# One core, attention into two mixture layers: the last sequence routed block by block, and work moved between engines inside the attention

## The chip, the cores and the metric

One Trainium2 chip, one of its cores. The metric is the device time of one execution in microseconds (us), lower is better. Times are compared as medians of runs of the same kernel.

## What is computed

Three layers in a row. The first is attention in which a query sees only the keys of its own cluster; the second sends every token to one of eight experts; the third is a dense two-matrix layer with a smooth gate. Cut from the reference:

```python
# attention: q, k, v (2, 8, 768, 64) fp32, 16 centroids per head
q_assign = np.argmax(np.einsum('bhsd,hcd->bhsc', q_n, c_n), axis=-1)   # the same for k
mask = q_assign[:, :, :, None] == k_assign[:, :, None, :]
scores = np.where(mask, scale * np.matmul(q, k.transpose(0, 1, 3, 2)), -1e9)
attn = np.exp(scores - np.max(scores, axis=-1, keepdims=True))
x = np.matmul(attn / (np.sum(attn, axis=-1, keepdims=True) + 1e-09), v)
# x becomes (1536, 512): 2 sequences of 768 tokens, 8 heads side by side
logits = x @ w_gate; expert_idx = np.argmax(logits, axis=1)            # 8 experts
# a token's place = how many earlier tokens went to its expert; dropped from 384 on
out[i] = gate_w[i] * (relu(x[i] @ w1[e]) @ w2[e])                      # 512 -> 1024 -> 512
# last layer: h = x @ w_in (512 -> 2048); g = h * tanh(softplus(h)); g @ w_out
```

## The kernel before

Almost all products are made of 16-bit halves: a value is a high part (fp16) and a low part (what is left), and a product is high times high, low times high and high times low. Some operations are there only to make such parts ("conversions").

**Attention.** There are 16 heads (8 of each sequence) and each head has two blocks of 384 queries, so 32 units u. A unit has three steps (z = 3u + t, 96 steps). For each unit: three score products against the keys that give the row maxima (`maxp`, line 663, copied out by ScalarE as `ev`, line 672, then halved three times, line 679, and reduced, line 683, on VectorE); the maxima are written into the queries and turned by a DMA transpose (`maxfin`, line 710, result `Q`); scores with the maxima in them (`scores`, lines 737 and 738) and their exponentials (line 745, `P`); the low parts of the exponentials (`plo`, line 762, `PL`), one operation for each of four key tiles; the weighted sum of the values (`av`, line 792, in PSUM as `pa`); the division and the split of the result into high and low (`avfin`, lines 815 to 831: `dn`, `x`, `xd`). For each head: the split of q, k and v (lines 517 to 564), the cluster choice (`cluster`, lines 592 to 627), of which `kmask` and `qmask` (lines 624 and 627) write the one-hot masks, and DMA transposes. All PSUM banks of these stages are in two rings, "s" (3 double banks) and "a" (2 banks).

**Routing.** After the last head pair of a block the token logits are put together from four head pairs: three by DMA transposes (`XT`, line 977, product in line 996, sum `LG` in lines 987 and 989), the last by transposes on TensorE (line 1008, copies `XTb` in line 1016, product in line 996, sum in line 1032). `plan_route` then chooses the expert (lines 1076 to 1080), counts places with small products (line 1096), computes the gate weight and the row number (`SLOT`, line 1103), and the Pool engine sends each group of 128 tokens to its row of `xs` in HBM by an indirect DMA (line 1130), six for a sequence. The first sequence is routed block by block while the second is in the attention. The second sequence is routed at the end, both its blocks (six groups) at once.

**One expert ahead.** 112 tokens of the largest expert of the first sequence are computed before the others (`go_ahead`: `phv` line 1597, `hv` lines 1602 and 1605, `pyv` line 1631, `yg` line 1553). Each weight piece (512 KB) is loaded as fp32 (`w1f`, `w2f`, line 1423), turned into a high part on ScalarE (line 1427) and a low part on VectorE (`wl`, line 1435). Eight pieces are needed, four of w1 and four of w2; two of w1 are asked for inside the attention's plan (at z = 86 and 89), the others after it. Then the eight experts follow (`ph` line 1470, `py` line 1515, tokens `xt` read back from `xs` by DMA transposes, line 1398), then the last layer (`fh` line 1785, `po` line 1873).

**What sets the order.** A planner written in the kernel takes the operations in the order of a list and gives each the first gap on its engine that fits, by durations written beside each operation; afterwards all are emitted in the order of their planned starts. So the position of every instruction on every engine is fixed before the program runs, and engines wait for each other by semaphores. The list is ordered by z plus or minus a lead per stage: `lm` (maxima) 8 steps ahead of the scores, `ls` 22, `lc` 16, `plo` 3 steps behind (`lp`), the sums 6 behind (`la`). `plan.best` takes the way that ends first by the planner's durations, after adding a bias. Where TensorE has a planned gap, small dummy products of 232 columns are put in (lines 462 and 466, `<-zero,ones`), and of 512 columns before the first expert (line 1479).

Of the kernel before, what the change touches and what calls it, by code (L numbers as in the profile page):

```python
# [9 lines left out]
F32 = mybir.dt.float32  # L10
# [34 lines left out]
    zs=2, zn=13, rest=300, lsl=1000.0, dsl=400.0, idur=100, iw=232, la=6, lm=8,  # L45
    lc=16, ls=22, ll=30, pt=1, r0=0.45, r1=50.0, nb=5, pb=3,
    qb=5, lp=3, profile=(320, 272, 240, 224, 192, 176, 160, 144), va=(112,), vbias=1000.0, ybias=1000.0, vf=3, vw=4,
    sbias=1000.0, plsl=30000, nl=1, abias=-20000.0, ol=2, wa=4, wb=4, vn=2,
    vz=86, vs=3, hsbias=500.0, obias=1000.0, nwi=4, nw=2, avw=225, fli=44, rsl=6000.0, lag0=5, lags=(), lasti=6, idl=30000, ask=2, pli=12, ob=4, pr=1.0, pr0=1.0, nwo=3, wo0=40, wos=8, hsl=200.0,
# [219 lines left out]
class Builder:  # L269
# [102 lines left out]
    def attention(self, ctx, rctx, pctx, plan, mkeep, extra, then):  # L372
# [200 lines left out]
        def cluster(i, part):  # L573
# [31 lines left out]
            else:  # L605
# [22 lines left out]

                def turn(nm, X, bufs):
# [8 lines left out]
                plan.op("DVE", 100, kmask, use=(e3, bf["KX0", i % nbuf]), add=KXb)  # L638
                plan.op("DVE", 100, qmask, use=(e3, bf["QX0", i % nbuf]), add=QXb)
# [6 lines left out]
        def maxp(u, t):  # L646
# [35 lines left out]
            def last():  # L682
                nc.vector.tensor_reduce(out=mkeep[:, u], in_=st["eh", u][:, :, 0:96], axis=AX.X, op=ALU.max)
# [8 lines left out]
            if t == 2:  # L692
                eh = Buf("eh", 2)
                plan.op("DVE", dve2(3 * 384), halve(384), use=bf["ev", u], new=eh)
                for n in (192, 96):
                    plan.op("DVE", dve2(3 * n), halve(n), use=eh, add=eh)
                plan.op("VEC", dve1(3 * 96), last, use=eh, new=bf["mk", u])
# [54 lines left out]
        def plo(u, pr):  # L752
            for j in range(2):
                kt = 2 * pr + j
                if kt >= NT - NW:
                    continue

                def emit(eng, kt=kt, j=j):
                    def f():
                        if ("PL", u) not in st:  # L760
                            st["PL", u] = late.tile([128, NT - NW, 384], F16, name="PL", tag="PL", bufs=P["pb"])
                        eng.tensor_tensor(out=st["PL", u][:, kt], in0=st["P32", u, pr][:, j], in1=st["PH", u, pr][:, j], op=ALU.subtract)  # L762
                    return f
                a, b = [("DVE", 470, emit(nc.vector))], [("POOL", 956, emit(nc.gpsimd))]
                plan.best(b, a, bias=P["pbias"], use=bf["P32", u, pr], new=bf["PL", u] if kt == 0 else None, add=bf["PL", u])
# [35 lines left out]
        def avfin(u):  # L801
# [4 lines left out]
            if h % 2 == 0 and blk == 0:  # L806
                self.XDb[b, pr] = (Buf(("XH", b, pr), 1), Buf(("XL", b, pr), 1))
            XHb, XLb = self.XDb[b, pr]
# [30 lines left out]
            if h == H - 1:  # L839
                def rest():  # L840
# [7 lines left out]
                    elif blk == BLK - 1:  # L848

                        self.plan_route(plan, b * BLK, BLK, self.small, ps)  # L850
                        self.plan_totals(plan, ps)
                later(rest, u)
            elif blk == BLK - 1:

                groups = [(0, 1, 2)] if b < B - 1 else [(0, 1), (2,)]
                for pairs in groups:
                    if pairs[-1] == pr:
                        fs = self.plan_gate(plan, b, late, ps, pairs=pairs)
                        for k, f in enumerate(fs):
                            later(f, u, k * P["gstep"] - P["defer"] if k < NT else max(0, (NT - 1) * P["gstep"] - P["defer"]))  # L860
# [80 lines left out]
    def plan_gate(self, plan, b, wk, ps, pairs=(), blk=None):  # L941
# [15 lines left out]
        else:  # L957
# [5 lines left out]
            for j in range(2):  # L963
                plan.op("PE", 165, turn[j], use=Xb[j], new=None if j else pm, add=pm)
            plan.op("ACT", act(384) + 55, copy[0], use=pm, new=XT)
            plan.op("VEC", dve1(384), copy[1], use=pm, add=XT)
# [31 lines left out]
    def gate_block(self, b, pr, blk, wk, ps, end):  # L998
# [12 lines left out]
        def copy(a):  # L1011
            def f():
# [3 lines left out]
                nc.vector.tensor_copy(out, src) if a else nc.scalar.activation(out=out, in_=src, func=AF.Copy)  # L1016
            return f

        def mm():
            if end:  # L1020
                pg = t["pm"][:, 0, w:w + 3 * E].rearrange("p (t e) -> p t e", t=3)
                self.pp = t["pm"][:, 1, w:].rearrange("p (t e) -> p t e", t=6)
# [1184 lines left out]
```

## Time and profile before

| | us |
|---|---|
| runs | 700.8, 695.21, 699.46 |
| median | 699.46 |
| profiled execution, its own time | 694.05 |
| span of the profiled execution | 692.3 |
| attention, from start to the last `pa` product | 0 to about 246.5 |
| routing of the last sequence and the expert ahead | 246.5 to 274.2 |
| eight experts | 274.2 to about 426 |
| last layer | 426 to the end |

Over the span TensorE is busy 93%, VectorE 80%, ScalarE 71% and Pool 10%. Busy time overlaps with waiting inside pipelined instructions, so a share says where to look and no more. In the profile PE is TensorE, DVE VectorE, ACT ScalarE, POOL the Pool engine (GpSimd) and SPq the queue of SyncE, which issues most DMAs; PEclk is the granted clock of TensorE, 1.00 for 2.4 GHz and 0.50 for 1.2 GHz.

### The profile page before, as it was taken

What the parts mean: (1) busy time and instruction counts of PE and PEld (TensorE: products, weight loads), DVE (VectorE), ACT (ScalarE), POOL (GpSimd) and SP (SyncE); (2) the same over time, 40 slices, a digit from 0 to 9 for tenths busy, and PEclk for the clock granted to TensorE, in tenths of its full rate; (3) what the DMA queues carried; (4) which work ended last, traced back from release to release, by engine and by line L of the source; (5) the groups of instructions that cost most, each with busy time, mean ns of one, the idle gap of its engine ahead of it and who ended that gap; (6) DMA issues with size and microseconds to landing.
All of it is one profiled execution on the core that took longest, in us unless ns stands there. A gap on an engine that the chain in (4) does not pass through costs nothing. (4 is left out here: it accounts for less than half of the span.)

```text
span 692.3 us, 15431 instructions
## 1 busy us (share of the span) xinstructions
PE 645.5 (93%) x6065; PEld 456.6 (66%) x6065; DVE 554.8 (80%) x1198; ACT 492.5 (71%) x717; POOL 67.2 (10%) x109
## 2 busy tenths in 40 slices
PE   7799999999998966999999999899999999999994
PEld 5576777777776864678999887454555555555541
DVE  6979979999998965788989996889888899545442
ACT  4479979978577723676667675889988878756760
POOL 3200000002200022012000000000260000001303
PEclk9989989999999998999999999999999999999998
DMA  6887999886566258999878992222333221000102
GB/s 176 159 149 191 240 252 226 154 154 190 125 148 106 67 196 254 318 326 295 259 246 257 246 313 95 92 91 62 91 61 94 62 92 32 0 1 16 76 1 95
DMA packets 148961, 103.96 MB, mean 150 GB/s; under 512 B 92304, under 2 KB 131216, under 8 KB 148880
## 3 DMA queue, kind: packets, MB, share of 16 engines
q1 hardware_dynamic: 146576, 96.21, 53.6%
q0 software_dynamic: 2304, 6.69, 2.6%
q8 instruction: 49, 0.80, 0.5%
q14 instruction: 32, 0.26, 0.1%
HBM read 64.02 MB, written 17.51 MB: 118 GB/s over the span
## 5 line engine op out<-in xcount | busy, mean ns | idle before, releaser
L1873 PEld LDWEIGHTS <-gt 128*128 128x128 f16 x576 | 56.3, 98 | 65.1
L745 ACT ACTIVATE P<-s 128x768 f32<-128x768 f32 x96 | 77.8, 812 | 28.6 <-PE s L738 22.5
L1873 PE MATMUL po<-xd,gt 128*128 128x512 f16 x432 | 97.0, 379 | 0.0
L1785 PE MATMUL fh<-x2h,winh 128*128 128x384 f16 x256 | 84.3, 329 | 4.9 <-DVE hs L1804 3.0
L1470 PE MATMUL ph<-xt,wh 128*128 128x320 f16 (+7 forms) x512 | 82.8, 259 | 3.3 <-DMA xt<-xs 3.3
L1785 PE MATMUL fh<-x2l,winh 128*128 128x384 f16 x256 | 84.2, 329 | 0.0
L1785 PE MATMUL fh<-x2h,winl 128*128 128x384 f16 x256 | 84.1, 329 | 0.0
L1515 PE MATMUL py<-ht,wh 128*128 128x320 f16 (+7 forms) x512 | 82.3, 256 | 0.1
L1785 PEld LDWEIGHTS <-winh 128*128 128x128 f16 x512 | 50.4, 98 | 41.9 <-issue 6.8
L672 ACT ACTIVATE ev<-pm 128x768 f16<-128x768 f32 x87 | 70.1, 809 | 7.5 <-PE pm L663 7.3
L737 PE MATMUL s<-Q,KXT 81*128 81x384 f16 x192 | 64.2, 335 | 7.8 <-DMA Q<-QX 5.4
L1470 PE MATMUL ph<-xt,wl 128*128 128x320 f16 (+7 forms) x256 | 64.4, 259 | 2.1 <-DVE wl L1435 2.1
L1515 PE MATMUL py<-ht,wl 128*128 128x320 f16 (+7 forms) x256 | 63.8, 256 | 1.4 <-DVE wl L1435 1.3
L738 PE MATMUL s<-QKT 128*128 128x384 f16 x192 | 64.1, 334 | 0.0
L762 DVE TENSOR_TENSOR PL<-P 128x384 f16<-128x384 f32 x119 | 61.8, 558 | 0.0
L792 PE MATMUL pa<-VW,P 128*128 128x65 f32 x384 | 59.6, 279 | 1.2 <-DVE LG L989 0.5
L792 PEld LDWEIGHTS pa<-VW,P 128*128 128x128 f32 x384 | 54.2, 198 | 8.0 <-issue 2.1
L1470 PEld LDWEIGHTS <-wh 128*128 128x128 f16 x512 | 48.0, 99 | 5.5 <-issue 0.4
L1515 PEld LDWEIGHTS <-wh 128*128 128x128 f16 x512 | 47.6, 98 | 4.9 <-issue 0.3
L792 PE MATMUL pa<-VX,P 128*128 128x65 f16 x768 | 49.6, 196 | 0.0
L663 PE MATMUL pm<-KXT,QXT 80*128 80x384 f16 x192 | 48.3, 335 | 0.8 <-ACT KXT L448 0.5
L792 PEld LDWEIGHTS <-P 128*128 128x128 bf16 x768 | 48.3, 106 | 0.0
(278 smaller groups left out, 1393.6 us busy)
## 6 DMA issues: line engine op xcount, KB each, us to landing
w1f<-in_moe_w_dram SPq DMA_DIRECT2D x36, 512.0 KB, 4.8
w2f<-in_moe_w_dram SPq DMA_DIRECT2D x36, 512.0 KB, 5.2
w2s<-in_moe_w_in_dram SPq DMA_DIRECT2D x16, 512.0 KB, 5.5
w2s<-in_moe_w_out_dram SPq DMA_DIRECT2D x16, 512.0 KB, 3.4
xs<-zero SPq DMA_DIRECT2D x13, 576.0 KB, 4.0
xsave<-xd SPq DMA_DIRECT2D x12, 256.0 KB, 4.3
kf<-in_k_dram SPq DMA_DIRECT2D x7, 384.0 KB, 4.4
qf<-in_q_dram SPq DMA_DIRECT2D x7, 384.0 KB, 4.8
```

The source lines that it names most:

```text
L663: nc.tensor.matmul(pm[:, j, 0:384], lhsT=QXT[0:80, g], rhs=KXT[0:80, 3 * j:3 * j + 3].rearrange("c t p -> c (t p)"), start=True, stop=True)
L672: nc.scalar.activation(out=st["ev", u][:, t].rearrange("p (a c) -> p a c", a=2), in_=st["pm", u, t][:, :, 0:384], func=AF.Copy, scale=1.0 ...
L737: nc.tensor.matmul(s[:, j, 0:384], lhsT=KXT[0:81, kt], rhs=Q2[0:81].rearrange("c t p -> c (t p)"), start=True, stop=False)
L738: nc.tensor.matmul(s[:, j, 0:384], lhsT=QKT[:, 1, kt], rhs=QKT[:, 0, 3 * blk:3 * blk + 3].rearrange("c t p -> c (t p)"), start=False, stop ...
L745: nc.scalar.activation(out=st["P32", u, pr], in_=st["s", u, pr][:, :, 0:384], func=AF.Exp, scale=sc)
L762: eng.tensor_tensor(out=st["PL", u][:, kt], in0=st["P32", u, pr][:, j], in1=st["PH", u, pr][:, j], op=ALU.subtract)
L792: nc.tensor.matmul(pa[:, t], lhsT=lhs, rhs=rhs, start=(n == 0), stop=(n == len(mm) - 1))
L1470: nc.tensor.matmul(st["p", i], lhsT=w[:, kk, fs], rhs=xt[:, 2 * kk + a], start=(kk == 0 and n == 0), stop=(kk == KD - 1 and n == 2))
L1515: nc.tensor.matmul(py, lhsT=w[:, f2, dsl], rhs=x, start=(f == 0 and j == 0), stop=(f == NF - 1 and j == 2))
L1785: nc.tensor.matmul(ph[b][:, 0:HB], lhsT=t2[w][:, f, k // 3], rhs=t2["x2"][x][:, k // 3, c0:c0 + HB], start=(k == 0), stop=(k == 3 * KD - 1))
L1873: nc.tensor.matmul(t2["o"][k], lhsT=gt[:, a, ts_], rhs=t2["wo"][f][:, w], start=(first and j == 0), stop=(last and j == 2))
```

## The change

- `plo` makes the low parts of two key tiles in one VectorE operation (768 elements instead of 384) and no longer has a way on Pool.
- The two masks of each head may go to ScalarE, with a bias that leaves them there unless it ends 1.5 us later.
- The maxima: `lm` 9 for 8; the last halving of 96 elements is dropped, and the reduction takes 192 instead of 96 elements for each of three rows. `plo` is placed 2 steps behind the scores for 3.
- The last sequence: each block has a route of its own (three groups), with its own dependency on the parts of `xd` that it reads. The copies `XTb` go to the engine that ends first.
- The expert ahead: four w1 pieces are placed in the attention (z = 80, 83, 86, 89), with five instead of four buffers for the parts; its first four products are planned ahead of the last route; the logits of the third head pair are placed half a step later.

```diff
-    ..., la=6, lm=8,
+    ..., la=6, lm=9,
-    qb=5, lp=3, ..., vw=4,
+    qb=5, lp=2, ..., vw=5,
-    ..., ol=2, wa=4, wb=4, vn=2,
-    vz=86, vs=3, ...
+    ..., ol=2, mbias=1500.0, glate=0.5, vpool=1000.0, ssl=0, wa=4, wb=4, vn=4,
+    vz=80, vs=3, ...
...
+                def kmask_a():
+                    nc.scalar.activation(out=KX[i % nbuf][:, :, 64:80], in_=st["e3", i][:, 1], func=AF.Copy, scale=KB, bias=-KB)
...
-                plan.op("DVE", 100, kmask, use=(e3, bf["KX0", i % nbuf]), add=KXb)
-                plan.op("DVE", 100, qmask, use=(e3, bf["QX0", i % nbuf]), add=QXb)
+                plan.best([("ACT", 190, kmask_a)], [("DVE", 100, kmask)], bias=P["mbias"], ...)
+                plan.best([("ACT", 190, qmask_a)], [("DVE", 100, qmask)], bias=P["mbias"], ...)
...
-                nc.vector.tensor_reduce(out=mkeep[:, u], in_=st["eh", u][:, :, 0:96], axis=AX.X, op=ALU.max)
+                nc.vector.tensor_reduce(out=mkeep[:, u], in_=st["eh", u][:, :, 0:192], axis=AX.X, op=ALU.max)
-                for n in (192, 96):
+                for n in (192,):
...
-            for j in range(2):
-                kt = 2 * pr + j
-                        eng.tensor_tensor(out=st["PL", u][:, kt], in0=st["P32", u, pr][:, j], in1=st["PH", u, pr][:, j], op=ALU.subtract)
-                a, b = [("DVE", 470, emit(nc.vector))], [("POOL", 956, emit(nc.gpsimd))]
-                plan.best(b, a, bias=P["pbias"], ...)
+            n = min(2, NT - NW - 2 * pr)
+                nc.vector.tensor_tensor(out=st["PL", u][:, 2 * pr:2 * pr + n], in0=st["P32", u, pr][:, 0:n], in1=st["PH", u, pr][:, 0:n], op=ALU.subtract)
+            plan.op("DVE", dve1(384 * n), emit, ...)
...
-                    elif blk == BLK - 1:
-                        self.plan_route(plan, b * BLK, BLK, self.small, ps)
-                        self.plan_totals(plan, ps)
-                later(rest, u)
+                    else:
+                        if blk == BLK - 1 and self.va:
+                            next(then)
+                        self.plan_route(plan, b * BLK + blk, 1, self.small, ps)
+                        if blk == BLK - 1:
+                            self.plan_totals(plan, ps)
+                later(rest, u, 3 * (NU - u) + P["la"] - P["defer"] - 2 if b == B - 1 and blk < BLK - 1 else 0)
...
-            plan.op("ACT", act(384) + 55, copy[0], use=pm, new=XT)
-            plan.op("VEC", dve1(384), copy[1], use=pm, add=XT)
+            for j in range(2):
+                plan.best([("ACT", act(384) + 55, copy(j, "ACT"))], [("VEC", dve1(384), copy(j, "VEC"))], ...)
```

What the order of the instructions became at three places. First TensorE, where the last unit's weighted sum (`pa`, from `P_4732` and `P_4677` before, line 792) stands against the logits of the third head pair (`pg`). Before, the end of the 18 `pg` products and the start of the last `pa`:

```order
L996 LDWEIGHTS XT
L996 MATMUL pg<-WG,XT 128x8
L792 MATMUL pa<-VW_169,P_4732 128x65 x2
L792 LDWEIGHTS P_4677
L792 MATMUL pa<-VX_163,P_4677 128x65
```

In the changed kernel, the end of the last `pa` and the start of `pg`:

```order
L795 MATMUL pa<-VX_163,P_4579 128x65
L795 LDWEIGHTS PL
L795 MATMUL pa<-VX_163,PL 128x65
L1002 LDWEIGHTS XT
L1002 MATMUL pg<-WG,XT 128x8
```

The 18 products moved from ahead of the last unit's sums to behind them. Second VectorE in the routing of the last sequence (`POS`, `OVER`, `rsf`, `SLOT` lead to the row numbers; `t...` are the totals of all experts; `hv` is the expert ahead). Before:

```order
L1099 TENSOR_TENSOR rpm<-pm,OH 128x48
L1121 CAST xd<-rsm 128x6
L1233 SCALAR_TENSOR_TENSOR tce<-pm,vc 128x8
L1122 TENSOR_TENSOR xd<-rsm,xd 128x6
L1100 TENSOR_REDUCE POS<-rpm 128x6
L1234 TENSOR_SCALAR tce<-tce 128x8
L1101 TENSOR_SCALAR OVER<-POS 128x6
L1235 TENSOR_TENSOR tkey<-tce,e_105 128x8
L1102 TENSOR_TENSOR rsf<-POS,rs_5007 128x6
L1103 TENSOR_TENSOR SLOT<-rsf,OVER 128x6
```

In the changed kernel, the end of the first block's route and the start of the second's:

```order
L1107 TENSOR_SCALAR OVER<-POS 128x3
L1127 CAST xd<-rsm 128x3
L1108 TENSOR_TENSOR rsf<-POS,rs_4822 128x3
L1128 TENSOR_TENSOR xd<-rsm,xd 128x3
L1109 TENSOR_TENSOR SLOT<-rsf,OVER 128x3
L1116 TENSOR_TENSOR CS<-CS,OH 128x8
L1082 TENSOR_REDUCE rmx<-LG 128x3
L1083 TENSOR_TENSOR re<-LG,rmx 128x24
L1084 TENSOR_TENSOR re<-re,w_103 128x24
L1612 SCALAR_TENSOR_TENSOR hv<-phv,hv 128x448
```

The row numbers of three groups now come before the second block's choice, and a second `SLOT` of three groups 14 instructions behind this piece. Third the DMA queue of SyncE at the end of the attention. Before:

```order
L1423 DMA w1f<-in_moe_w_dram 128x4x256
L710 DMA_TRANSPOSE Q_4553<-QX_150 128x3x128
L977 DMA_TRANSPOSE XT<-xd 128x2x128 x6
L1423 ISA
L1423 DMA w2f<-in_moe_w_dram 128x2x512
L1423 ISA
L1423 DMA w2f<-in_moe_w_dram 128x2x512
L1137 DMA xsave<-xd 128x1024 x6
L1423 ISA
L1423 DMA w2f<-in_moe_w_dram 128x2x512
```

In the changed kernel:

```order
L1429 DMA w2f<-in_moe_w_dram 128x2x512
L716 DMA_TRANSPOSE Q_4427<-QX_150 128x3x128
L1429 ISA
L1429 DMA w2f<-in_moe_w_dram 128x2x512
L1429 ISA
L1429 DMA w2f<-in_moe_w_dram 128x2x512
L983 DMA_TRANSPOSE XT<-xd 128x2x128 x6
L1143 DMA xsave<-xd 128x1024 x6
L1429 ISA
L1429 DMA w2f<-in_moe_w_dram 128x2x512
```

Three of the four w2 pieces are asked for ahead of the last logits' transposes, and one is left behind the saves, where two were.

## Rows read from the trace of the kernel before

**Rows 1.** windows: us, then busy us (instructions) of PE, PEld, DVE, ACT, POOL; PEclk, DMA, GB/s

```profile
40.00:246.00 206.00, 197.07 (x2602) 156.50 (x2601) 186.86 (x575) 165.52 (x271) 12.16 (x12) 0.97 0.76 168
246.00:274.17 28.17, 16.63 (x272) 14.14 (x272) 19.45 (x60) 9.83 (x15) 7.85 (x6) 0.94 0.70 231
274.17:692.30 418.13, 399.44 (x2889) 263.00 (x2888) 317.24 (x477) 296.75 (x388) 37.46 (x27) 0.99 0.45 135
35.60:42.00 6.40, 6.40 (x47) 3.98 (x45) 5.03 (x16) 4.96 (x9) 0.00 (x0) 0.50 0.67 122
90.00:96.40 6.40, 6.34 (x56) 5.41 (x54) 4.96 (x15) 3.44 (x7) 0.00 (x0) 0.50 1.03 271
```

**Rows 2.** VectorE groups by shape, 20 to 246: count, busy us, mean ns, idle before

```profile
L762 DVE TENSOR_TENSOR PL<-P 128x384 f16<-128x384 f32 x119 | 61.8, 558 | 0.0
...
L683 DVE TENSOR_REDUCE mkeep<-eh 128x3 f32<-128x288 f16 x29 | 13.1, 453 | 0.7
L831 DVE TENSOR_TENSOR xd<-x,xd 128x192 f16<-128x192 f32 x31 | 11.5, 371 | 2.0 <-ACT xd L828 2.0
...
L679 DVE TENSOR_TENSOR eh<-eh 128x288 f16<-128x288 f16 x29 | 8.9, 307 | 0.8
L666 DVE TENSOR_REDUCE mkeep<-pm 128x1 f32<-128x768 f32 x9 | 8.3, 950 | 1.6 <-PE pm L663 1.6
...
L624 DVE TENSOR_SCALAR KX<-e 128x96 f16<-128x96 f16 x15 | 2.8, 188 | 0.5
```

**Rows 3.** VectorE in order of time: start us, us, what, count

```profile
234.34 1.96 DVE L762 TENSOR_TENSOR PL<-P 128x384 f16<-128x384 f32 x4
...
238.29 0.98 DVE L831 TENSOR_TENSOR xd<-x,xd 128x192 f16<-128x192 f32 x1
```

**Rows 4.** Pool in order of time

```profile
238.20 0.86 POOL L762 TENSOR_TENSOR PL<-P 128x384 f16<-128x384 f32 x1 [54.52 <-ACT P L745]
254.76 1.00 POOL L1130 DMA_INDIRECT xs<-xd,SLOT  x1 [15.70 <-DVE trk L1240]
...
257.35 2.16 POOL L1130 DMA_INDIRECT xs<-xd,SLOT  x1 [0.30 <-issue]
...
261.10 1.75 POOL L1130 DMA_INDIRECT xs<-xd,SLOT  x1 [0.30 <-issue]
263.15 0.98 POOL L1130 DMA_INDIRECT xs<-xd,SLOT  x1 [0.30 <-issue]
```

**Rows 5.** ScalarE groups by shape, 20 to 246

```profile
L564 ACT ACTIVATE VW<-vf 128x128 f32<-128x128 f32 x12 | 3.9, 325 | 3.4 <-DMA vf<-in_v_dram 3.4
```

**Rows 6.** waits of TensorE, 40 to 246: us in total, times, longest

```profile
PE s L737 <- DMA Q<-QX: 5.4, 5, 1.4
```

**Rows 7.** TensorE in order of time

```profile
242.72 0.59 PE L996 MATMUL pg<-WG,XT 128*128 128x8 f16 x18
243.83 0.63 PE L792 MATMUL pa<-VW,P 128*128 128x65 f32 x4 [0.52 <-DVE LG L989]
...
246.32 0.19 PE L792 MATMUL pa<-VX,PL 128*128 128x65 f16 x1
...
268.77 2.10 PE L1479 MATMUL ph<-zero,ones 128*128 128x512 f16 x9 [0.54 <-DVE yg L1553]
274.17 0.42 PE L1470 MATMUL ph<-xt,wh 128*128 128x320 f16 x1 [3.29 <-DMA xt<-xs]
```

**Rows 8.** VectorE in order of time, routing of the last sequence

```profile
253.82 0.17 DVE L1103 TENSOR_TENSOR SLOT<-rsf,OVER 128x6 int32<-128x6 f32 x1
...
257.45 1.21 DVE L1435 SCALAR_TENSOR_TENSOR wl<-w2f,wh 128x1024 f16<-128x1024 f32 x1
```

**Rows 9.** ScalarE in order of time

```profile
247.73 1.06 ACT L1427 ACTIVATE wh<-w2f 128x1024 f16<-128x1024 f32 x1
248.91 0.95 ACT L1016 ACTIVATE XTb<-pm 128x384 f16<-128x384 f32 x2
```

**Rows 10.** the SyncE queue in order of time

```profile
269.98 2.99 SPq L1398 DMA_TRANSPOSE xt<-xs  x2
```

More of the change, by code (lines that the diff above doesn't have):

```diff
@@ L859, in avfin @@
                         for k, f in enumerate(fs):
[L860 removed]
+                            later(f, u, k * P["gstep"] - P["defer"] if k < NT else max(0, (NT - 1) * P["gstep"] - P["defer"]) + (P["glate"] if b == B - 1 and pr == self.KD - 2 else 0))
         bf["CT"] = Buf("CT", 1)
@@ L963, in plan_gate @@
             for j in range(2):
-                plan.op("PE", 165, turn[j], use=Xb[j], new=None if j else pm, add=pm)
-            plan.op("ACT", act(384) + 55, copy[0], use=pm, new=XT)
-            plan.op("VEC", dve1(384), copy[1], use=pm, add=XT)
+                plan.op("PE", 165, turn[j], use=Xb[2 * blk + j], new=None if j else pm, add=pm)
+            for j in range(2):
+                plan.best([("ACT", act(384) + 55, copy(j, "ACT"))], [("VEC", dve1(384), copy(j, "VEC"))], use=pm, new=None if j else XT, add=XT)
             plan.op("PE", 260, mm, use=(XT, self.WGb, *((pm,) if end else ())), new=None if end else pg, add=pg)
@@ L1015, in f @@
                 out, src = t["x"][:, a].rearrange("p t c -> p (t c)"), t["pm"][:, a, 0:384]
-                nc.vector.tensor_copy(out, src) if a else nc.scalar.activation(out=out, in_=src, func=AF.Copy)
+                nc.vector.tensor_copy(out, src) if eng == "VEC" else nc.scalar.activation(out=out, in_=src, func=AF.Copy)
             return f
@@ L1032, in add @@
             nc.vector.tensor_tensor(out=LG, in0=t["pg"], in1=LG, op=ALU.add)
-        return (turn(0), turn(1)), (copy(0), copy(1)), mm, add
+        return (turn(0), turn(1)), copy, mm, add
     def plan_route(self, plan, n, m, wk, ps):
@@ L1056, in plan_route @@
         for g in range(3 * n, 3 * n + 3 * m):
-            plan.dma("POOL", 830, lambda g=g: self.dispatch(g, self.XD[b]), use=(gw, placed, self.CLb, *(x for pr in range(self.KD) for x in self.XDb[b, pr])),
+            plan.dma("POOL", 830, lambda g=g: self.dispatch(g, self.XD[b]), use=(gw, placed, self.CLb, *(x for pr in range(self.KD) for x in self.XDb[b, pr][2 * (n % self.NB):2 * (n % self.NB + m)])),
                      add=(self.XSb, *((self.XS0b,) if b < self.B - 1 else ())), slack=self.cfg["slack"] if n < self.NB else 0.0)
@@ L1451, in weights @@
             s = [("ACT", act(n), scale_a), ("POOL", pool2(n), low_p)]
-            wb = P["vbias"] if r < nv else P["wbias"] if r > nv or c or part else 0.0
+            wb = (P["vpool"] if c >= P["vn"] and not part else P["vbias"]) if r < nv else P["wbias"] if r > nv or c or part else 0.0
             plan.best(a, b, s, bias=(wb, wb + P["sbias"]), use=(wf, wh), new=wl)
@@ L1581, in go_ahead @@
             hv, Y, y = {}, [], []
+            floor = plan.floor
             NQ = 4
@@ L1944, in second_half @@
             plan.floor = t0 + 2.0
-            end = go_ahead()
+            end = yield from go_ahead()
             plan.floor = 0.0
```

46 lines of the change are left out of this document (26 added, 20 removed).

## The prediction

> **What bounds the kernel now.** I first read the busy time by stretch [rows 1]: in each row the busy microseconds of TensorE, VectorE and ScalarE stand against the length. From 274.17 on TensorE is busy 399.4 of 418.1 us. The matrix work there is the same before and after, so I expect that stretch to move as a whole. In the attention (40 to 246) TensorE shows 197.1 of 206, but part of that is dummy products, and VectorE shows 186.9: it is idle for only 19.1 us. So there two engines are nearly full, and VectorE is the one whose work is all needed. Between 246 and 274.17 TensorE is busy 16.6 of 28.2 us: this is the routing of the last sequence, and nothing else in the kernel has such a hole.
>
> Then I followed that hole backwards from its end. The first product of the experts starts at 274.17 after 3.29 us of waiting for the tokens read back from HBM [rows 7]. That read was issued at 269.98 [rows 10], when the last of six indirect DMAs had landed; Pool issued the six from 254.76 on, the last at 263.15 for 0.98 us, that is to 264.13 [rows 4]. The first could start once VectorE had the row numbers, at 253.82 + 0.17 = 253.99 [rows 8]. These in turn hang on the last sum of the attention, which ended at 246.32 + 0.19 = 246.51 [rows 7]. So the hole is 7.5 us of routing, 0.8 to the first issue, 9.4 of issuing, 5.8 of landing and 4.2 for the read. Last I looked for waits in the attention: five waits of the scores for their turned queries, 5.4 us in all [rows 6], and the clock, which stood at 0.50 for two stretches of 6.4 us, 35.6 to 42 and 90 to 96.4 [rows 1].
>
> **The change, part 1: VectorE in the attention.** Durations overlap with the next instruction: a `PL` of 384 elements takes 558 ns alone [rows 2], but four in a row 1.96 us [rows 3]. Four at a pace p with a last one of 0.558 give p = (1.96 - 0.558) / 3 = 0.47, so about 0.09 of a duration is hidden; I take it off everywhere. An element costs (950 - 453) / (768 - 288) = 1.04 ns in the two reductions [rows 2].
> - Pairs: 119 operations at 0.47 = 55.9 us go, 64 at 0.47 + 384 x 0.00104 = 0.87 come, 55.7 us. This is -0.2, though nine that ran on Pool are now in it.
> - Masks: 32 operations at 0.188 - 0.09 = 0.10 [rows 2] leave: -3.2.
> - Maxima: 29 halvings at 0.307 - 0.09 = 0.22 go (-6.4), 29 reductions grow by 288 x 1.04 ns = 0.30 (+8.7): +2.3.
> - Two more w1 conversions, of the size of the `wl` of 1.21 [rows 8], at 1.12: +2.2. They leave the hole, where they would have cost nothing if the tokens are last.
> - Four low parts of `xd` go to Pool: 4 x (0.371 - 0.09) [rows 2] = -1.1. Some six copies come back from ScalarE, for which I take 0.15 each, between the mask's 0.10 and the 0.47 of a `PL`: +0.9.
> - The nine `PL` leave Pool. One of them, at 238.20, lies beside a VectorE low part that took 0.98 [rows 3, 4] where the mean is 0.371 [rows 2]: 0.6 us lost. I count two such meetings among the nine: -1.2.
>
> The sum is -0.2 - 3.2 + 2.3 + 2.2 - 1.1 + 0.9 - 1.2 = -0.3 us: VectorE has as much to do as before. So the attention can only gain what is idle now, 19.1 us at most, and no change of work gives it.
>
> ScalarE takes 32 masks. No row has a 96-element activation; 128 elements take 325 ns [rows 5], nothing shorter than a VectorE mask (188 ns) is likely, so 3 to 10 us of busy time, I take 7. ScalarE is idle for 206 - 165.5 = 40.5 us in the attention, which covers it; if it is full at that moment a mask is late, and with it one DMA transpose, for which the list now leaves 7 steps ahead of the maxima (16 less 9) where it left 8.
>
> What may use the idle time is the order. A step is 206 / 87, about 2.4 us; the maxima run one step earlier, and each of the five waits for turned queries is 1.4 at most [rows 6]. They would go, but VectorE worked all through most of them, so it is late next. The order shows the same thing from the other side: behind the first six steps 55 dummy products of 232 columns are left of 106, and 232 columns at 2.4 GHz are 0.1 us. So the plan has about 5 us less of TensorE gaps. I take half of either figure, -2.5, and keep both ends: -9.5 (half of VectorE's idle time goes) and +2.5 (nothing is gained, and the added conversions show).
>
> **Part 2: the hole.** The last unit's sum started at 243.83, behind 18 gate products at 242.72 and a wait of 0.52 [rows 7]. Now they stand behind it: -1.1. ScalarE did a w2 conversion of 1.06 us ahead of the two copies that the last logits need, at 247.73 and 248.91 [rows 9]; now the copies stand ahead: -0.7. The route of the first block has its row numbers before the second block's choice and before the totals, about ten small operations of 0.08 earlier (a `SLOT` takes 0.17 less the hidden 0.09 [rows 8]): -0.8. So the first indirect DMA starts about 2.6 us earlier. The second block's numbers are some 3 us behind the first's, because an `hv` and its wait stand between; the first three issues take 3 x 1.3 us or more, so these cover it. If they didn't, issue four would wait, at most 1 us. Six issues still follow each other, so the whole chain moves by 2.6 us: the split in blocks gains a head start, not a shorter row of issues. The landing stays at 5.8: half a megabyte less of weights is loaded beside it, but the last three pieces still are.
>
> On the cost of these issues the rows show that four of six took about 1 us, but that at 257.35 took 2.16 and that at 261.10 1.75 [rows 4], the first beside a `wl` of 1.21 at 257.45 [rows 8]. The change puts three `wl` of w2 in a row behind the totals, just where the last three issues fall, so a third such meeting can come: 2.16 - 0.98 = 1.2 more. I keep that as an end of the range and take two meetings, as now.
>
> The Trainium skill, page "SBUF — State Buffer", section "Who interferes with whom", speaks against my choice: VectorE and GpSimd share one pair of ports under an exclusive lock, and a VectorE operation with two inputs in SBUF, as `wl` is, and a GpSimd operation that reads SBUF block each other for a whole instruction. By that rule all three meet, and the hole gains 1.4 instead of 2.6. So far two issues of six were long [rows 4], which is why I stay with two.
>
> The w2 chain must not become last. Before, it ended where the dummies begin, at 268.77, 5.4 us ahead of 274.17 [rows 7]. Now its first `wl` comes some 2 us later behind the last sum, since the second block's route stands ahead of it; but three of four pieces are there by then, and one load and one conversion follow it instead of two. So I let its end move with the last sum alone, 1.1 us earlier, while the route gains 2.6: of the 5.4 us of cover 3.9 are left. The chain stays hidden, but a load that lands 4 us late would take the place of the route.
>
> **Sum.** 694.05 for the profiled execution (span 692.3 and 1.75 around it). -2.5 for the attention, -2.6 for the hole, 0 behind it: 688.95, which is 0.7% less. The median of the runs is 699.46, 0.8% above the profiled one; scaled, 699.46 x 688.95 / 694.05 = 694.3.
>
> **The rivals.**
> - *The order fits much better.* Half of VectorE's idle time goes, with one of the two stretches at half clock: -9.5 - 2.6 = -12.1, 687.4. For it: at 90 to 96.4 VectorE itself worked only 4.96 of 6.4 us, so a slow TensorE starves it, and a wait for turned queries precedes that stretch. Against: VectorE has no less to do.
> - *Nothing arrives.* The order's gain goes into the conversions, and in the hole the w2 chain or a held issue takes the place of the route: 699.5. For it: only 3.9 us of cover over the w2 chain. Against: the gate products and the copy did stand in the path.
> - *TensorE falls to half clock more often.* With half of the dummies gone and VectorE as full as before, TensorE stands idle where it was kept busy; a stretch at 0.50 of 6.4 us costs 3.2 of its work [rows 1]. Three more of them in the attention give +9.6 - 2.6 = +7: 706.5. It decides from the first one on, since one eats the hole's gain. For it: both stretches shown follow idle time of TensorE. Against: most waits of similar length had no such stretch behind them.
>
> **How the numbers follow.** My forecast 0.46 (its own range 690 to 698.5), the better order 0.26, nothing 0.17, the clock 0.11. A measurement of this kernel tells about 1%, 7 us. Faster by more: nearly all of the second case and a fifth of the first, 0.34. Slower by more: half of the clock's case and a little of the third, 0.08. The rest, 0.58, is within 1%. The range leaves out half of the better order's lower part and most of the clock's case: 685 to 704.
>
> **What would show it.** Right: the last `pa` is followed by `pg` and starts without a wait; the first indirect DMA starts 6.5 to 7 us behind the last sum (8.25 before) and the sixth ends 16 behind it (17.6); the first expert product waits for the tokens; VectorE's busy time in the attention is within 2 us of before. Wrong: the first expert product waits for a `wl` or a `yg` instead; the fourth issue waits for `SLOT`; more than two stretches at 0.50 between 40 and the end of the attention; or the attention's end moves by more than 6 us either way.

## The result and the profile after

The changed kernel takes 688.53 us in the median of six runs (686.66 to 695.72), the kernel before 699.92 (695.21 to 700.8). The ratio is 0.9883 with a 95% interval of 0.9842 to 0.9925, so it is faster by 1.2%. Run again later, beside 13 other runs of the kernel before, the same kernel had 0.9854 (0.9766 to 0.9942). Each ratio, here and below, leaves out runs more than 1.5% above the fastest of their kernel, which takes out five of the ten runs of singles_vector, two of the five of before_leads and one each of singles_back, fill_ten and totals_split (in before_leads, singles_back and totals_split the profiled one is among them).

The profiled execution took 687.50 us (span 685.6) against 694.05: 6.55 less. The rows below show where this lies, by the same stretches as before. Columns are start and end, length, busy microseconds (and instructions) of TensorE, weight loads, VectorE, ScalarE and Pool, then the granted clock of TensorE, the DMA share and GB/s. First the kernel before, from 20 us to the last sum:

```profile
20.00:246.51 226.51, 214.24 (x2785) 168.52 (x2784) 204.71 (x616) 176.49 (x292) 15.72 (x17) 0.96 0.75 166
```

and the changed kernel:

```profile
20.00:239.60 219.60, 207.74 (x2733) 161.78 (x2734) 198.53 (x504) 178.16 (x317) 10.96 (x10) 0.98 0.81 176
239.60:268.11 28.51, 17.16 (x265) 15.84 (x262) 20.31 (x79) 8.65 (x15) 8.83 (x6) 0.80 0.58 190
268.11:685.60 417.49, 399.91 (x2889) 263.59 (x2888) 317.17 (x477) 297.61 (x389) 36.02 (x26) 0.98 0.46 135
```

The last sum ends 6.91 earlier (239.60 for 246.51, of which 1.1 are the gate products that now stand behind it). The hole up to the first expert product is 28.51 long, where it was 274.17 - 246.51 = 27.66: 0.85 longer. The stretch behind it is 0.64 shorter (417.49 for 418.13, [rows 1]). VectorE's idle time up to the last sum hardly moved, 219.60 - 198.53 = 21.1 for 21.8. Its work fell by 6.2.

The waits of TensorE between 40 and 238 (total, times, longest):

```profile
PE pl L592 <- DMA QKT<-QK: 3.1, 2, 1.6
PE s L743 <- DMA Q<-QX: 1.8, 2, 1.0
```

The five waits for turned queries, 5.4 us [rows 6], became two of 1.8 in all; two waits of the cluster products for a transpose are new, 3.1 in all.

VectorE's groups by shape, 20 us to the last sum (count, busy, mean ns, idle before):

```profile
L767 DVE TENSOR_TENSOR PL<-P 128x768 f16<-128x768 f32 x64 | 60.7, 951 | 0.0
L689 DVE TENSOR_REDUCE mkeep<-eh 128x3 f32<-128x576 f16 x29 | 21.8, 753 | 0.7
L834 DVE TENSOR_TENSOR xd<-x,xd 128x192 f16<-128x192 f32 x27 | 9.5, 350 | 0.5 <-ACT xd L831 0.4
```

They answer to [rows 2]: 64 pairs stand for 119 single low parts, and the reduction is 0.300 longer, as forecast. The masks on ScalarE:

```profile
L630 ACT ACTIVATE KX<-e 128x96 f16<-128x96 f16 x15 | 4.2, 281 | 7.9 <-DVE e L621 7.8
L633 ACT ACTIVATE QX<-e 128x96 f16<-128x96 f16 x15 | 4.0, 268 | 0.0
```

The hole, TensorE in order of time (start, length, what, count, the wait ahead of it), answering to [rows 7]:

```profile
239.41 0.19 PE L795 MATMUL pa<-VX,PL 128*128 128x65 f16 x1
239.44 0.59 PE L1002 MATMUL pg<-WG,XT 128*128 128x8 f16 x18
...
264.56 0.38 PE L1485 MATMUL ph<-zero,ones 128*128 128x512 f16 x1 [1.78 <-DVE yg L1559]
268.11 0.43 PE L1476 MATMUL ph<-xt,wh 128*128 128x320 f16 x1 [3.17 <-DMA xt<-xs]
```

Pool in order of time, answering to [rows 4]:

```profile
247.41 0.99 POOL L1136 DMA_INDIRECT xs<-xd,SLOT  x1 [25.43 <-DVE re L1084]
248.71 0.98 POOL L1136 DMA_INDIRECT xs<-xd,SLOT  x1 [0.30 <-DVE rm L1085]
250.00 0.98 POOL L1136 DMA_INDIRECT xs<-xd,SLOT  x1 [0.30 <-issue]
251.66 0.98 POOL L1136 DMA_INDIRECT xs<-xd,SLOT  x1 [0.68 <-issue]
252.94 0.98 POOL L1136 DMA_INDIRECT xs<-xd,SLOT  x1 [0.31 <-DVE ttmp L1235]
254.22 3.93 POOL L1136 DMA_INDIRECT xs<-xd,SLOT  x1 [0.30 <-issue]
```

and VectorE, answering to [rows 8]:

```profile
246.38 0.16 DVE L1109 TENSOR_TENSOR SLOT<-rsf,OVER 128x3 int32<-128x3 f32 x1
...
253.82 3.47 DVE L1441 SCALAR_TENSOR_TENSOR wl<-w2f,wh 128x1024 f16<-128x1024 f32 x3
```

The first indirect DMA starts 247.41 - 239.60 = 7.81 behind the last sum, for 8.25. The first five issues take 0.98 or 0.99. The sixth takes 3.93, beside three conversions in a row, and ends 18.55 behind the last sum, for 17.62: the head start is given back there.

One thing is needed to read the numbers that follow. Single executions of one kernel differ, and the longer ones show more time of TensorE at half clock. What a whole run loses by it is its span times (1 - granted clock). In 29 runs of the kernel before, made beside the first eight experiments, this is 21.6 us in the mean, with a mean span of 698.2, and a run with 1 us more of it was 0.60 us longer (a straight line through the 29; 0.45 and 0.73 in its two groups of 16 and 13). The profiled execution of before lost 692.3 x 0.023 = 15.9 and was shorter than every one of the 29 (694.2 to 703.4). In ten runs of the changed kernel the mean is 20.0 lost and a span of 688.3, with a slope of 0.73.

### The profile page after: what moved, and what is told of

It reads as the page before. It is cut to its first block, busy times and chain, and to the rows that moved or that the text cites. A ratio compares the mean times of both kernels' runs of the same rounds, so it can differ in the third digit from the quotient of the medians.

```text
span 685.6 us, 15230 instructions
## 1 busy us (share of the span) xinstructions
PE 639.4 (93%) x6011; PEld 451.9 (66%) x6011; DVE 549.3 (80%) x1104; ACT 494.5 (72%) x744; POOL 62.7 (9%) x103
## 5 line engine op out<-in xcount | busy, mean ns | idle before, releaser
L767 DVE TENSOR_TENSOR PL<-P 128x768 f16<-128x768 f32 x64 | 60.7, 951 | 0.0
L795 PE MATMUL pa<-VW,P 128*128 128x65 f32 x384 | 57.0, 271 | 0.8 <-DVE e L600 0.4
L795 PEld LDWEIGHTS pa<-VW,P 128*128 128x128 f32 x384 | 52.6, 191 | 6.0 <-PE pt L1171 0.8
L1433 ACT ACTIVATE wh<-w2f 128x1024 f16<-128x1024 f32 x36 | 37.8, 1051 | 17.3 <-DMA w2f<-in_moe_w_dram 16.0
L795 PE MATMUL pa<-VX,P 128*128 128x65 f16 x768 | 48.2, 194 | 0.0
```

The source lines that it names most:

```text
L767: nc.vector.tensor_tensor(out=st["PL", u][:, 2 * pr:2 * pr + n], in0=st["P32", u, pr][:, 0:n], in1=st["PH", u, pr][:, 0:n], op=ALU.subtract)
L795: nc.tensor.matmul(pa[:, t], lhsT=lhs, rhs=rhs, start=(n == 0), stop=(n == len(mm) - 1))
L1433: nc.scalar.activation(out=t["h"], in_=t["f"], func=AF.Copy, scale=SW)
```

## The experiments

Two theories stood after the result. **A**: VectorE's work sets the pace of the attention, and the gain is the 6.2 us of work. **B**: the order sets it, and the gain is the maxima that run one step earlier. For the hole: Pool's issue waits for conversions that began before it, or the sixth issue is long for a reason of its own.

**same_again**: the changed kernel, once more.

> The changed kernel itself once more. The attention of totals_earlier has the same order up to its last sum and ended 2.9 us later (242.50 against 239.60), with more time at half clock; ScalarE stood 3.0 us ahead of the copy gb there, and 0.6 here. If these are a matter of the execution: the last sum somewhere between 239 and 243, the stall of ScalarE ahead of gb either 0.6 or 2.5 to 3.0, and the time within 687 to 696. If they belong to the kernels: 239.6 and 0.6 again, to 0.5.

Measured: last sum 244.53, ScalarE 1.1 us ahead of `gb`, ratio 0.9854 (0.9766 to 0.9942). So the execution decides several microseconds of where the attention ends. The place where much of it is decided can be shown. In the changed kernel, one wait, and the stretch behind it:

```profile
138.90 0.76 PE L592 MATMUL pl<-CT,QKT 128*128 128x16 f16 x24 [1.53 <-DMA QKT<-QK]
```

```profile
140.80:144.00 3.20, 3.20 (x12) 1.62 (x11) 2.05 (x6) 2.59 (x5) 0.00 (x0) 0.50 0.60 135
```

the same place in same_again, and its attention:

```profile
20.00:244.53 224.53, 212.18 (x2733) 165.07 (x2734) 198.69 (x504) 178.46 (x318) 10.97 (x10) 0.95 0.79 172
141.20:154.80 13.60, 13.41 (x137) 10.51 (x138) 10.07 (x24) 7.31 (x14) 0.00 (x0) 0.50 0.85 179
```

and in totals_earlier, which has the same order up to the last sum:

```profile
20.00:242.50 222.50, 209.28 (x2733) 162.17 (x2734) 198.51 (x504) 177.71 (x318) 10.97 (x10) 0.97 0.79 174
140.40:147.20 6.80, 6.76 (x49) 3.69 (x50) 4.43 (x11) 4.21 (x8) 0.00 (x0) 0.51 0.82 210
```

These are the same instructions with the same 198.5 to 198.7 us of VectorE's work and the same wait ahead (1.53, 1.75 and 1.53), and stretches at 0.50 of 3.2, 6.8 and 13.6 us; the last sum comes at 239.60, 242.50 and 244.53. They reach this place at 138.90, 140.44 and 139.76, so most of the 4.9 us of same_again and about half of the 2.9 of totals_earlier arise behind it. So a last sum is read with its half-clock time beside it, and 5 us of one prove nothing. VectorE's work, though, is the same in all three, so that can be compared.

**masks_back**:

```diff
-                plan.best([("ACT", 190, kmask_a)], [("DVE", 100, kmask)], bias=P["mbias"], use=...)
+                plan.op("DVE", 100, kmask, use=...)
```

and the same for `qmask`.

> The changed kernel with the two masks of each head back on VectorE. Theory A (VectorE's work sets the pace of the attention; its idle time between 20 us and the last sum stays at 21 to 22 us): VectorE gets back 3.1 us, the last sum ends at about 242.7 instead of 239.6, the time is about 691.6. Theory B (the order decides: the maxima one step earlier took the waits away): the last sum stays within 1 us of 239.6 and the time at 688.5.

```profile
20.00:243.79 223.79, 210.43 (x2756) 163.13 (x2754) 202.76 (x536) 174.30 (x291) 9.27 (x8) 0.98 0.78 173
```

VectorE has 4.2 us more, its idle time is 21.0, and the last sum stands 4.2 later, at 243.79, with the granted clock no lower than in the changed kernel. The profile is as A has it. The ratio, 0.994 (0.990 to 0.9979), is some 4 us slower than the changed kernel's 0.9883, but the two intervals overlap a little, so the times alone don't show it.

**singles_back** (the low parts by single operations of 384, with their way on Pool, as before) and **singles_vector** (the same, all on VectorE):

```diff
-            plan.op("DVE", dve1(384 * n), emit, use=bf["P32", u, pr], ...)
+                a, b = [("DVE", 470, emit(nc.vector))], [("POOL", 956, emit(nc.gpsimd))]
+                plan.best(b, a, bias=P["pbias"], use=bf["P32", u, pr], ...)
```

> The changed kernel with the low parts in single operations of 384 again, with their way on Pool. Theory A with a price for Pool: some 5 to 10 low parts go to Pool, the small VectorE operations beside them (xd, QX, dn) and the 1152-element halving get longer by 3 us in all, and the last sum ends 2 to 3 us later, time about 691. If pairs and Pool cost nothing (the sum of my prediction gave 1.4 for both together): last sum within 1.5 us, time 688.5 to 690.

> The changed kernel with single low parts of 384, all on VectorE, none on Pool. singles_back (16 of them on Pool) took 12 us more than the changed kernel and showed 25 us at half clock lost ahead of the last sum. If Pool's share makes that (its low parts take 0.8 us or more, late for the sums, and TensorE waits): within 3 us of the changed kernel. If it is the single operations (8 more operations of 0.47 for every 4 pairs cost little, but the order differs): 697 or more again.

singles_back: 18 low parts on Pool, 201.72 us of VectorE's work up to the last sum, ratio 1.0027 (0.9995 to 1.0058): the whole gain is gone. singles_vector, with no low part on Pool:

```profile
20.00:243.61 223.61, 209.39 (x2752) 162.01 (x2750) 203.24 (x565) 180.08 (x326) 10.20 (x9) 0.98 0.79 173
```

VectorE has 4.7 us more than in the changed kernel (128 singles at 0.47 are 60.2, where 64 pairs take 55.8, counted from start to next start) and is idle for 20.4; the ratio is 0.9926 (0.9881 to 0.997). So Pool's share alone isn't it, and both expectations missed in size. But Pool's way saves VectorE little: 18 low parts of 0.47 are 8.5 us less, and its work fell by 1.5 only. In part more copies fell to VectorE, but most of it is that what stands beside Pool's low parts gets longer. The plainest group, VectorE in singles_back:

```profile
L530 DVE COPY KX<-QK 128x384 f16<-128x384 f16 x8 | 4.7, 589 | 0.0
```

and in singles_vector:

```profile
L530 DVE COPY KX<-QK 128x384 f16<-128x384 f16 x5 | 1.3, 255 | 0.0
```

Five of the eight copies in singles_back lie beside a low part on Pool and took 0.72 to 0.81, the three others 0.25. One such pair, which ends 0.11 apart:

```profile
102.45 2.03 POOL L769 TENSOR_TENSOR PL<-P 128x384 f16<-128x384 f32 x1 [10.14 <-ACT P L751]
```

```profile
103.78 0.81 DVE L530 COPY KX<-QK 128x384 f16<-128x384 f16 x1
```

Of the two ways to do single low parts Pool's looks the dearer, by ratios whose intervals don't overlap. But singles_vector's ratio is of the shorter half of its runs. Over all ten runs of each, the medians are 703.2 for singles_back (699.7 for the kernel before beside it) and 699.39 for singles_vector (699.96), and the means of the half-clock time are 30.2 and 23.0 us. At 0.60 for each of these, an estimate, the 7 us make 4 us, about the whole distance between the two. Why Pool's way comes with more half clock isn't shown.

**leads_back**:

```diff
-    ..., la=6, lm=9,
-    qb=5, lp=2, ...
+    ..., la=6, lm=8,
+    qb=5, lp=3, ...
```

> The changed kernel with the maxima 8 steps ahead and the low parts 3 steps behind, as before. Theory A: VectorE's work is the same to 1 us, the last sum within 1.5 us of 239.6, time 687 to 690. Theory B (order): waits of the scores for their turned queries come back (5 of them, about 5 us against 1.8 in two now), last sum 3 to 5 us later, time 692 to 694.

```profile
PE s L743 <- DMA Q<-QX: 9.0, 9, 2.1
```

```profile
20.00:249.98 229.98, 214.32 (x2776) 169.29 (x2777) 202.15 (x506) 180.62 (x322) 6.71 (x6) 0.97 0.75 168
```

There are nine waits for turned queries instead of two, and VectorE is idle for 27.8 us: with the old leads it is starved, and A alone doesn't explain this. Its work up to the last sum is also 3.6 more. The last sum is 10 us later in the profile. The ratio, 0.9898 (0.9864 to 0.9932), overlaps with the changed kernel's; the median is 693.8. B has a part, then: the pairs and masks need the longer lead, by this profile.

**before_leads** and **before_pairs_leads**, the kernel before with the leads alone, and with leads and pairs.

> The kernel before with the leads alone (maxima 9 steps ahead, low parts 2 behind). If the leads carry the gain in the attention: the waits for turned queries fall from 5.4 to about 2 us, the last sum ends at 241 to 243 (246.5 before), time about 695. If they need the pairs (leads with single low parts were the slowest so far, 703): last sum at 247 or later, time 700 to 704.

> The kernel before with pairs and leads, nothing else. If the two together carry the attention's gain: last sum at 241 to 243, hole as before (27.7), time about 695. If the masks are needed too (VectorE has 3 us more): last sum 244 to 246, time 697 to 699.

The ratios are 0.9899 (0.9806 to 0.9991) for before_leads, from three runs, and 0.9908 (0.9868 to 0.9948) for before_pairs_leads. The profiled execution of before_leads is a long one, 704.03, with three stretches of 13.6 us at half clock and the last sum at 247.68, so it says little on the attention. That of before_pairs_leads:

```profile
20.00:244.61 224.61, 210.32 (x2777) 164.05 (x2775) 204.01 (x569) 173.82 (x289) 8.36 (x7) 0.98 0.77 168
```

VectorE's work is hardly less than before's 204.71, and the last sum is 1.9 earlier. So the order brings a part without work saved, and the work another: masks_back and before_pairs_leads both lie between the two kernels. Much of the order's part is half clock: the ten runs of before_pairs_leads lost 16.7 us by it in the mean and the 13 of the kernel before beside them 22.3, which at 0.60 is 3.4 us (an estimate) of the 6.9 between their mean spans. The parts can't be added up, and the intervals don't say which is larger.

For the profiles the two theories can be told apart all the same. In seven of them (the changed kernel, masks_back, singles_vector, before_pairs_leads, and fill_ten, fill_waits and all_three further down), all with the new leads, no stretch at half clock between 20 us and the last sum is longer than 3.6 us. In these the last sum less VectorE's work from 20 us on is between 40.4 and 41.4, while the work itself goes from 198.5 to 204.0. So with the new leads, and without a long stretch at half clock, the last sum follows VectorE's work nearly one to one. The kernel before has 41.8 with two stretches of 6.4: of the 6.91 that the change gained there, 6.2 are work and 0.7 idle time. That less half clock made the gain (0.98 for 0.96) is ruled out as far as single profiles can do it, since masks_back and before_pairs_leads stand at 0.98 too.

**totals_earlier** and **totals_split**, for the hole. The second half of the totals is asked for earlier, whole or its first five operations:

```diff
-    ... rsl=6000.0, ...
+    ... rsl=2000.0, ...
```

```diff
-        self.chain(plan, self.COLb, [("DVE", *o) for o in rest], use=(pt, self.METAb), slack=self.cfg["rsl"])
+        self.chain(plan, self.COLb, [("DVE", *o) for o in rest[:5]], use=(pt, self.METAb))
+        self.chain(plan, self.COLb, [("DVE", *o) for o in rest[5:]], use=(self.COLb, self.METAb), slack=self.cfg["rsl"])
```

> The changed kernel with the second half of the totals asked for earlier, so that one w2 conversion stands ahead of them on VectorE instead of three. If an issue of Pool that begins beside a conversion waits for the end of the run of conversions and then takes its 0.98: the sixth issue takes 1.7 to 1.9 us instead of 3.93, the first expert product starts about 2.1 us earlier against the last sum (26.4 instead of 28.5), time about 686.5. If the sixth issue is long for a reason of its own (its queue, its place): it stays at 3.5 to 4 and nothing moves.

> The changed kernel with five small operations of the totals ahead of the three w2 conversions in a row, so that the sixth issue of Pool begins before the first of them. If an issue is held only by a conversion that began before it: the sixth issue takes 0.98 instead of 3.93, and the first expert product comes 1 to 2.5 us earlier against the last sum (26 to 27.5 instead of 28.4), where the w2 chain becomes last. If a conversion holds an issue at any time: 3 us or more again.

In totals_earlier one conversion stands ahead of the sixth issue:

```profile
259.10 1.20 DVE L1441 SCALAR_TENSOR_TENSOR wl<-w2f,wh 128x1024 f16<-128x1024 f32 x1
```

```profile
259.50 1.66 POOL L1136 DMA_INDIRECT xs<-xd,SLOT  x1 [0.30 <-issue]
```

With the edit of totals_split, here from all_three below, the issue begins first and three conversions follow:

```profile
257.12 0.98 POOL L1136 DMA_INDIRECT xs<-xd,SLOT  x1 [0.30 <-issue]
```

```profile
257.44 3.49 DVE L1441 SCALAR_TENSOR_TENSOR wl<-w2f,wh 128x1024 f16<-128x1024 f32 x3
```

The issue ends 0.86 behind the run of conversions that it found under way: at 258.15 in the changed kernel (run until 253.82 + 3.47 = 257.29), at 261.16 in totals_earlier (run until 260.30). The two long issues of the kernel before fit: they end at 259.51 and 262.85, each 0.85 behind a run of two and of one. If the issue begins before the run, it takes 0.98 and the conversions aren't longer. That the reason was its place is refuted. By the Trainium skill, page "SBUF — State Buffer", section "Who interferes with whom", a VectorE operation with two inputs in SBUF contends with a Pool operation that reads SBUF, for a shared port under an exclusive lock; the rows agree, and add that a run of conversions back to back lets nothing in between. The section also infers that `tensor_tensor` leaves the making of DMA descriptors alone; for `scalar_tensor_tensor`, as here, and an indirect DMA the rows show otherwise.

The gain reached the experts in small part: the first product of theirs came 27.80 behind the last sum in totals_earlier, for 28.51; the ratios are 0.9864 (0.9818 to 0.9909) and, for totals_split, 0.9839 (0.9775 to 0.9904). One reason lies ahead of the sixth issue. The fourth came 4.06 us behind the third, for 1.66 in the changed kernel:

```profile
256.93 0.98 POOL L1136 DMA_INDIRECT xs<-xd,SLOT  x1 [3.08 <-issue]
```

So the sixth issue, though 2.3 shorter, ended 18.66 behind the last sum and no earlier than before the edit (18.55). The last section comes back to this wait. The other reason is the w2 chain, with two of its conversions now behind the totals: `yg` ends at 270.03, and the first expert product starts at 270.30, so an earlier route would have gained little more.

**fill_ten**, ten dummies for one ahead of the first expert, and **fill_waits**, dummies in the two new waits of the cluster products:

```diff
-                    nc.tensor.matmul(st["idle"], ...)
+                    [nc.tensor.matmul(st["idle"], ...) for _ in range(10)]
```

```diff
-                    pl = st["pl", i]
+                    pl = st["pl", i]; [idle_work(bf["pl", i]) for _ in range(12 if i in (9, 11) else 0)]
```

> The changed kernel with ten dummy products of 512 columns for one ahead of the first expert, in the 3.2 us that TensorE waits for the tokens. The changed kernel's first expert ran at half clock from 268.1 to 273.9. If that costs its full price: the clock is at 1.00 there, the stretch from the first expert product to the end takes 414.6 instead of 417.5, time about 685.6. If the first experts wait for weights and conversions anyway (leads_back had 21 dummies and full clock there and took 416.9): 417, time within 1 us of the changed kernel's.

> The changed kernel with twelve dummy products of 232 columns ahead of the cluster products of two heads, where TensorE waited 1.5 us for a DMA transpose at 112 and at 139 and a stretch at half clock began right after, in all four profiles of this order (3.2 to 13.6 us long). If these waits bring the stretches: none at 113 and 141, the last sum at 236 to 238.5, time about 685 to 687 with less spread. If they come from something else: stretches at the same places, last sum 240 to 245 as before.

fill_ten: the clock is 1.00 from 268.05 to 274, where the changed kernel had 0.51, and the stretch from the first expert product to the end takes 684.7 - 268.05 = 416.65 for 417.49. But same_again has 415.98 without the dummies, with the clock at 0.72 in the first 6 us. So half clock costs the first expert nothing that can be told from chance. The ratio is 0.9789 (0.970 to 0.9878), which overlaps with the changed kernel's.

fill_waits: the stretch behind the second of the waits is gone.

```profile
138.00:148.00 10.00, 9.72 (x163) 7.84 (x162) 7.53 (x20) 7.46 (x15) 0.00 (x0) 1.00 1.12 207
```

None is left between 20 us and the last sum, which still ends at 240.14 and not at 236 to 238.5:

```profile
20.00:240.14 220.14, 207.34 (x2761) 161.96 (x2759) 199.38 (x507) 177.52 (x318) 10.97 (x10) 1.00 0.82 175
```

Short stretches of 3.2 us are covered, then (three in the changed kernel, 239.60); it is the long ones that a kernel pays for. The expectation has the stretches in all four profiles of this order; at 113 us totals_earlier had none, behind a shorter wait of 0.96. Behind the sum, the gate products waited:

```profile
243.44 0.23 PE L1002 MATMUL pg<-WG,XT 128*128 128x8 f16 x3 [2.66 <-DMA XT<-xd]
```

With this wait, and with a fourth issue 4.20 behind the third, the hole of this execution is 34.54 long instead of 28.51, and its time 694.85; whether the edit brings that isn't shown, as the three other runs took 686.84 to 691.92. The ratio is 0.9861 (0.9791 to 0.9932).

**all_three**: fill_waits, totals_split and fill_ten together.

> Both edits above and the ten dummies ahead of the first expert together. If they add up: last sum at 236 to 238.5, first expert product 26 to 27.5 behind it, time about 684. If what is saved is waited for elsewhere: 686 to 689.

The last sum is at 239.91 and the first expert product 30.63 behind it: the fourth issue came 4.19 behind the third, the sixth ended 18.19 behind the sum (18.55 in the changed kernel), `yg` ends at 268.3, and now the ten dummies stand behind it until 270.5. The ratio is 0.9845 (0.9781 to 0.9908). The four runs lie close together, 686.79 to 689.54, with 12.3 us lost at half clock in the mean for 20.0, but no version was faster than the changed kernel by more than the intervals.

## Why the prediction was right, and where it was wrong

The range of 685 to 704 held the result, and the direction was right. The number, 694.3, was 5.8 too high, outside the 690 to 698.5 of the likeliest case and near the 687.4 of the better order. For the profiled execution, -5.1 was forecast and -6.55 measured, and that is luck in good part: the last sum came 6.91 earlier where the forecast gives 3.6 (2.5 and the gate products' 1.1), and the hole behind it, forecast 1.5 shorter, was 0.85 longer. By its own signs the prediction missed too: VectorE's work moved by more than 2 us, the attention's end by more than 6, the first indirect DMA and the sixth were later than said. By its steps:

- **The scale** ("0.8% above the profiled one; scaled"). The medians differ by 11.4, the profiled executions by 6.55. The scaling by 0.8% took the distance between the profile and the median as the kernel's; it was 5.4 us before and 1.0 after. The profiled execution of before had lost 15.9 at half clock, a usual run 21.6, and at 0.60 each that is 3.4 of the 5.4. This step failed, and it makes 4.3 of the 5.8: the distance belonged to that execution.
- **VectorE's work**, forecast -0.3, was -6.1, with each operation counted from its start to the next start, or to its own end if that comes first. Masks -3.1 (forecast -3.2) and the low parts of `xd` -2.3 (Pool's four and the end of Pool's low parts, -1.1 and -1.2) came as worked out. Pairs gave -1.1 (-0.2), since the single low parts had taken 0.478 each and not 0.47. Nine operations came back from ScalarE for +2.0 (forecast: six for +0.9). The maxima were mis-sized: forecast +2.3, measured +0.4. The reductions grew by 8.5, as forecast (8.7), but the 29 halvings were worth 8.1 and not 6.4. Where the reduction of the same data stood behind a halving (19 of 29) the next start was 0.342 later, which is its own 0.307 and a gap; where another operation did, 0.226. So the 0.09 taken off every operation was wrong for those 19. The conversions gave +1.0 for +2.2: three of the four already stood ahead of the last sum before. The last -3.0 is spread over many groups, a little shorter each; singles_back, where 18 low parts on Pool made VectorE's other work some 7 us longer, says that the nine before can have cost this.
- **"The attention can only gain what is idle now"** failed with it: the idle time stayed at 21 us, and the work went. The rival of the better order had the time almost right, but not the sum (-12.1 against -6.55) and not the reason: half of VectorE's idle time was to go.
- **The waits for turned queries** went as forecast, from five to two, and leads_back, with nine, shows that the leads did it; before_leads and before_pairs_leads have 1.2 and 1.6 us of them.
- **ScalarE** took 30 masks for 8.2 us (7 forecast for 32), and of TensorE's waits in the attention none names a mask; two short ones for `QXT`, which the masks go into, are new (0.7).
- **The hole**, forecast -1.5 behind the last sum, was +0.85. The first issue came at 7.81, not 6.5 to 7: TensorE ran the first products of the expert ahead at half clock (243.2 to 246.4), ahead of the counts of the first block. Of the six issues one alone met conversions, not two or three, but three in a row: it took 2.95 more than the usual, where the two long ones before had cost 1.95 together. The fourth stood 0.4 longer than the usual gap. So the sixth ended 18.55 behind the sum, not 16. For the forecast a meeting cost 1.2 at most; a row of conversions was not in it. The rule of the Trainium skill's page, in the section named above, pointed the right way with its smaller gain of 1.4 for 2.6, but by another count of meetings.
- **The w2 chain** stayed hidden behind the tokens (a wait of 3.17), and totals_earlier and all_three show how thin the cover was.
- **The clock's rival** did not come for the changed kernel. But its mechanism is real: behind one place, where a stretch was 10.4 us longer, the last sum of the same kernel came some 4 us later.

## What to carry to other kernels

Before a time is scaled from one profile to a median, set the profile's lost clock time beside that of the other runs; here the profiled execution of before was shorter than all 29 others. Where an engine is nearly full, add up its work from start to next start, group by group, rather than with one constant for overlap, and watch its idle time: if that stays when the work changes, as in seven profiles here, work is what counts. A Pool issue should begin before a run of two-input VectorE operations, not behind its first one; but look first at which chain is next behind it.

## What the runs showed that was not expected

A stretch at 1.2 GHz behind the same wait at the same place lasted 3.2, 6.8 or 13.6 us in three executions. The short ones cost the attention nothing that shows (239.60 with three of them, 240.14 with none); what decides the length stayed open.

ScalarE stood still ahead of `gb` for 0.56 us in the changed kernel and for 3.0 in totals_earlier, although the instructions ahead are the same and `pgb`, the product that it reads, started 1.23 behind the start of the last `wh` in both:

```profile
249.35 0.26 ACT L1546 ACTIVATE gb<-pgb 128x112 f32<-128x112 f32 x1 [0.56 <-ACT wh L1433]
```

```profile
254.68 0.26 ACT L1546 ACTIVATE gb<-pgb 128x112 f32<-128x112 f32 x1 [2.99 <-issue]
```

"issue" says that the profile names nothing it waited for. The second block's gate weights stand behind it, so the fourth indirect DMA came 4.06 behind the third there and 1.66 in the changed kernel. The wait was 0.56 in fill_ten, 1.14 in same_again, and 2.6 to 3.2 in masks_back, singles_vector, fill_waits and all_three, with the fourth issue 4.2 behind the third in these four. So the changed kernel's own hole of 28.51 was read from an execution with the short wait, and holes of single profiles can't be compared without it. No run was made for this, and its cause is open.
